# A fixed order for every engine up to the first feed-forward step of an attention and mixture kernel

## The chip, the cores and the metric

The kernel runs on one core of one Trainium2 chip. The metric is device time in microseconds of one execution. A core has a matrix engine (TensorE, PE in the profile; PEld is its weight load), VectorE (DVE), ScalarE (ACT), GpSimd (POOL) and SyncE (SP), which here only issues DMAs. Each engine works through its own list of instructions in order; semaphores hold an instruction back until what it needs is done.

## The reference, cut to what matters

```python
def _attn_ref(q, k, v, mem_k, mem_v):            # (4, 8, 768, 64), 8 memory rows
    for c in range(24):                          # chunks of 32 queries
        k_full = concat(mem_k, k[c_start - 16:c_end + 8])     # cut at both ends
        scores = scale * q_c @ k_full.T
        a = exp(scores - max(scores)); a = a / (sum(a) + 1e-09)
        out[:, :, c_start:c_end] = a @ v_full

def _moe_ref(x, w_in, w_out, s, b):              # x (3072, 512), d_ff 2048
    r = maximum(x @ w_in, 0.0)
    return (s * (r * r) + b) @ w_out

def _moe2_ref(x, phi, w1, w2):                   # 8 experts of 4 slots
    logits = x @ phi
    slot_input = softmax(logits, axis=0).T @ x
    slot_out[e] = maximum(slot_input[e] @ w1[e], 0.0) @ w2[e]
    return softmax(logits, axis=1) @ slot_out
```

The weights w_in and w_out arrive in 64-bit floats and are turned into 32-bit ones on the chip.

## The kernel before

The 3072 tokens are worked in six blocks j of 512 tokens. The attention of a block is four units, one for each pair of heads, so unit u is pair u % 4 of block u // 4. A unit is a chain over all engines: `spread_q` (S, first block only: the two heads of q are copied to where their zeros have been cleared, one half of the partitions by ScalarE, one by VectorE), `att_qk` (A: 32 matmul records into one bank, then VectorE clears masked columns of that bank), `att_soft` (F: row maximum and subtraction on VectorE, exponential on ScalarE, row sum, epsilon and reciprocal on VectorE, the normalising multiply on Pool in the start and on VectorE later), `att_tr` (T or t: four transposes on PE, two copies into `pb`), `att_pv` (P: matmuls with v, then x's high part on ScalarE and its low part on VectorE).

The feed-forward part takes 96 steps n, 16 a block; step n works on slice f = n % 16 of d_ff. `mm_h` multiplies x with wi, `make_g` makes s r^2 + b, `mm_y` multiplies it with wo. Each fp32 operand is split into a high and a low part (`split_wi`, `split_wo`: ScalarE rounds, VectorE subtracts in the first 16 steps, Pool later), and a product is three passes: high x high, high x low, low x high. In the first block each half of a weight slice is also decoded from 64 bits: `w_load` brings a half (512 KB) into a staging tile; `w_decode` clamps it on VectorE, makes two pieces on ScalarE and joins them on VectorE. The halves come in the order (0, 0), (0, 1), (1, 0), ..., where (f, 0) is wi and (f, 1) is wo of slice f. `START` decodes some halves, and steps 0 to 13 two each. mm_h(n) needs half (n, 0), mm_y(n) needs (n, 1).

`START` is a string of tokens: q, k, v, c and w load; z issues warm-up products for PE that nothing reads; I is `split_wi`; H is one quarter of step 0's `mm_h`; D decodes one half; y hands four spent tiles to the staging list, and w9 loads halves into all that is free. Everything stands in `tc.manual_schedule` for PE and SP: these two keep the order in which the code issues. The order on ScalarE, VectorE and Pool is made by a planner at build time, which takes the code's order as priority and a model of durations for when things are ready; on the chip that order is fixed. After `START` come steps 0, 1, ...: splits for the next step, `mm_h`, `make_g`, two decodes, the attention of the next block (`bg`, from step 1 on) and `mm_y` of the step before. So the quarter H3, in step 0, and `mm_h(1)` follow the start on PE, then A4, the scores of unit 4, the first of the next block.

## Time and profile before

| | us |
|---|---|
| median of three runs | 697.64 (697.57 to 698.52) |
| profiled execution | 697.7 |
| its span on the core | 695.9 |
| PE busy | 675.7 |
| DVE busy | 357.7 |
| ACT busy | 353.6 |
| POOL busy | 216.7 |

The profile's times are counted from the start of the span; 1.8 us of the execution lie around it. PE's first instruction starts at 1.31 us. Busy time of PE is that of pipelined matmuls, whose ends are modelled. The granted clock of PE is a share of 2.4 GHz and stands at 0.5 or 1.0 at any moment; a stretch shows the mean. Engines other than PE have idle time that costs nothing as long as PE doesn't wait for them.

### The profile page before, as it was taken

To read this page: it belongs to the slowest core of one execution; us is meant where nothing else is said; L and a number is where in the kernel's file an instruction comes from. 1 tells how busy PE (TensorE), PEld (TensorE's weight loads), DVE (VectorE), ACT (ScalarE), POOL (GpSimd) and SP (SyncE) were. 2 spreads that over 40 slices of the span, in tenths; PEclk is the share of its full clock that TensorE was granted. 3 is DMA by queue.
4 is the path that set the end of the run, shared out by engine and by line. 5 is a ranking of instruction groups with operands and counts; after the bars stand their busy time and mean duration, and the time that the engine had idled before them with its cause. 6 is when DMAs were issued, how large, how long until landed. Compare 5 with 4: busy or idle time off the path is not lost.

```text
span 695.9 us, 12228 instructions
## 1 busy us (share of the span) xinstructions
PE 675.7 (97%) x4953; PEld 533.3 (77%) x4953; DVE 357.7 (51%) x644; ACT 353.6 (51%) x628; POOL 216.7 (31%) x178
## 2 busy tenths in 40 slices
PE   7599999999999999999999999999999999999995
PEld 4488888888788888788888788888788888787353
DVE  5689997446534456544445444554553332223233
ACT  4779894544444445444445444545444544444332
POOL 4100000343344334334434334434334444441000
PEclk9799999999999999999999999999999999999998
DMA  9998802702201211211120221120123523628998
GB/s 348 389 336 328 270 40 91 284 32 80 91 16 77 91 42 50 91 52 64 68 75 18 91 67 56 61 91 1 62 84 129 211 92 91 211 92 272 237 294 348
DMA packets 47032, 94.38 MB, mean 136 GB/s; under 512 B 2944, under 2 KB 27520, under 8 KB 46976
## 3 DMA queue, kind: packets, MB, share of 16 engines
q1 hardware_dynamic: 46976, 93.60, 39.3%
q8 instruction: 39, 0.64, 0.4%
q14 instruction: 17, 0.14, 0.1%
HBM read 87.30 MB, written 6.29 MB: 134 GB/s over the span
## 4 chain that ended last, share of the span: by engine, by line
PE 95%; DVE 2%; ACT 1%; POOL 1%; issue 0%; POOLq 0%; DVEq 0%; ACTq 0%
PE bank L292 39%; PE bank L272 38%; PE bank L221 4%; PE bank L181 3%; PE bank L686 2%; PE bank L643 2%; PE bank L207 2%; PE bank L336 1%; PE bank L712 1%; PE bank L314 1%; PE bank L352 1%; PE bank L504 1%; PE bank L390 0%; POOL rt L201 0%; PE bank L662 0%
## 5 line engine op out<-in xcount | busy, mean ns | idle before, releaser
L292 PE MATMUL bank<-g,wo 128*128 128x512 f32 x1152 | 285.2, 396 | 0.0
L272 PE MATMUL bank<-x,wi 128*128 128x512 f32 x1152 | 278.6, 391 | 0.0
L272 PEld LDWEIGHTS bank<-x,wi 128*128 128x128 f32 x1152 | 217.1, 189 | 45.2
L292 PEld LDWEIGHTS bank<-g,wo 128*128 128x128 f32 x1152 | 211.1, 188 | 48.9 <-ACT wi L259 4.2
L279 DVE SCALAR_TENSOR_TENSOR rt<-bank,cons,rt 128x512 f32<-128x512 f32 x96 | 72.0, 750 | 228.3 <-ACT rt L278 228.1
L265 POOL TENSOR_TENSOR wo<-w,wo 128x512 fp32r<-128x512 f32 x80 | 103.2, 1290 | 204.9 <-ACT wo L264 200.9
L260 POOL TENSOR_TENSOR wi<-w,wi 128x512 fp32r<-128x512 f32 x80 | 103.4, 1293 | 188.8 <-ACT wi L259 188.8
L259 ACT ACTIVATE wi<-w 128x512 fp32r<-128x512 f32 x96 | 60.5, 630 | 148.3 <-PE bank L272 144.8
L280 ACT ACTIVATE g<-rt,cons 128x512 fp32r<-128x512 f32 x96 | 69.4, 723 | 42.6 <-DVE rt L279 41.3
L264 ACT ACTIVATE wo<-w 128x512 fp32r<-128x512 f32 x96 | 60.3, 628 | 55.2 <-PE bank L292 53.5
L281 DVE SCALAR_TENSOR_TENSOR g<-rt,cons,g 128x512 fp32r<-128x512 f32 x96 | 72.0, 750 | 27.3 <-ACT g L280 24.5
L278 ACT ACTIVATE rt<-bank 128x512 f32<-128x512 f32 x96 | 55.8, 581 | 5.4 <-PE bank L272 5.2
L197 ACT ACTIVATE ep<-ep 128x512 f32<-128x512 f32 x22 | 13.8, 627 | 30.1 <-DVE ep L196 30.1
L221 PEld LDWEIGHTS bank<-pb,v 128*64 128x64 f32 x704 | 22.3, 138 | 7.1 <-issue 6.7
L181 PEld LDWEIGHTS bank<-k,q 128*64 128x64 f32 x704 | 22.4, 138 | 5.6 <-issue 4.5
L181 PE MATMUL bank<-k,q 128*64 128x64 f32 x704 | 24.7, 223 | 1.7 <-ACT ep L197 1.7
L221 PE MATMUL bank<-pb,v 128*64 128x64 f32 x704 | 25.3, 225 | 0.0
L198 DVE TENSOR_REDUCE ast<-ep 128x8 f32<-128x512 f32 x22 | 15.1, 685 | 9.8 <-ACT ep L197 9.7
L225 DVE TENSOR_TENSOR x<-bank,x 128x512 fp32r<-128x512 f32 x24 | 16.5, 688 | 0.6 <-ACT x L224 0.5
L224 ACT ACTIVATE x<-bank 128x512 fp32r<-128x512 f32 x24 | 14.3, 596 | 4.9 <-PE bank L221 2.5
L195 DVE TENSOR_REDUCE ast<-bank 128x8 f32<-128x512 f32 x24 | 16.4, 683 | 0.4
L199 DVE TENSOR_SCALAR ast<-ast 128x8 f32<-128x8 f32 x24 | 15.9, 664 | 0.7
(237 smaller groups left out, 522.6 us busy)
## 6 DMA issues: line engine op xcount, KB each, us to landing
k<-kd SPq DMA_DIRECT2D x22, 512.0 KB, 6.1
sp<-wd SPq DMA_DIRECT2D x22, 512.0 KB, 8.8
v<-vd SPq DMA_DIRECT2D x22, 512.0 KB, 3.9
q<-qd SPq DMA_DIRECT2D x20, 512.0 KB, 5.3
w<-e1d SPq DMA_DIRECT2D x10, 512.0 KB, 3.4
out<-w SPq DMA_DIRECT2D x9, 512.0 KB, 6.2
sp<-e1d SPq DMA_DIRECT2D x7, 512.0 KB, 7.9
sp<-e2d SPq DMA_DIRECT2D x7, 512.0 KB, 7.2
```

Of the source, the lines that this page charges most:

```text
L181: pe.matmul(S[64 * par:64 * par + 64, 2 * i + z, :], lhsT=qt[:, c].rearrange("p h n -> p (h n)"), rhs=kt[:, c, :], start=True, stop=True)
L221: pe.matmul(b[64 * h:64 * h + 64, 64 * m:64 * m + 64], lhsT=vt[:, m, h, :], rhs=pb[:, m // 2, m % 2, h].rearrange("p z n -> p (z n)"), sta ...
L259: act.activation(out=r32(t[:, 0]), in_=raw, func=AF.Copy)
L260: (dve if n < NF else pool).tensor_tensor(out=r32(t[:, 1]), in0=raw, in1=t[:, 0], op=ALU.subtract)
L264: act.activation(out=r32(t[:, 0]), in_=raw, func=AF.Copy)
L265: (dve if n < NF else pool).tensor_tensor(out=r32(t[:, 1]), in0=raw, in1=t[:, 0], op=ALU.subtract)
L272: pe.matmul(HB[n % 2], lhsT=r32(w[:, a, kt, :]), rhs=r32(x[:, b]), start=(kt == 0 and i == 0), stop=(kt == 3 and i == 2))
L278: act.activation(out=r, in_=HB[n % 2], func=AF.Relu, scale=1.0 / WSCALE ** 2)
L279: dve.scalar_tensor_tensor(out=t, in0=HB[n % 2], scalar=s_col, in1=r, op0=ALU.mult, op1=ALU.mult)
L280: act.activation(out=r32(g[:, 0]), in_=t, func=AF.Identity, bias=b_col)
L281: dve.scalar_tensor_tensor(out=r32(g[:, 1]), in0=t, scalar=b_col, in1=g[:, 0], op0=ALU.add, op1=ALU.subtract)
L292: pe.matmul(YB[dt], lhsT=r32(w[:, a, dt * 128:dt * 128 + 128]), rhs=r32(g[:, b]), start=(f == 0 and i == 0), stop=(f == NF - 1 and i == 2))
```

## The change

The start's order is now fixed on ScalarE, VectorE and Pool too: the loop over the tokens stands in a second `manual_schedule` for these three, inside the one for PE and SP. Where instructions from outside the region (steps 0, 1, ...) fall among those of the region is still the planner's. To make the order finer, several functions are cut in two: `att_soft` into `att_exp` (m: clears, maximum, subtraction, exponential) and `att_norm` (n: sums and multiply), with the clears moved out of `att_qk` into m; x's low part out of `att_pv` into `att_low` (x); `w_decode` into `w_begin` (D: clamp and ScalarE's pieces) and `w_end` (E: the join); `split_wi` into `wi_high` (I) and `wi_low` (i). The VectorE half of S1, S2 and S3 moves to Pool. T0 now copies with ScalarE alone, T3 with ScalarE and VectorE. One warm-up product of the three at the start goes, and the others stand elsewhere. Halves of weights are loaded and decoded in the order (0, 0), (1, 0), (0, 1), (2, 0), (1, 1), (3, 0), .... The start decodes four halves, as before; w9 now comes after the last of them.

```diff
--- before.py
+++ after.py
@@ -22,9 +22,9 @@
 NEG = -3.0e38
 EPS = 1e-9
 START = (
-    "q0 k0 w1 c0 q1 k1 q2 k2 v0 w1 q3 k3 v1 w1 v2 v3 w1 "
-    "z3 S0 A0 F0 z1 S1 D0 A1 z1 S2 t0 z1 A2 P0 F1 S3 T1 F2 "
-    "I0 A3 k4 w1 q4 w1 k5 P1 v4 w1 T2 q5 H0 P2 F3 T3 P3 y0 H1 w9 H2 D0 v5 D0 D0"
+    "q0 k0 q1 k1 w1 c0 q2 k2 v0 q3 k3 v1 w1 v2 w1 v3 w1 "
+    "z2 S0 A0 z1 S1 A1 m0 n0 D0 S2 m1 A2 E0 T0 I0 n1 S3 m2 z1 P0 T1 A3 i0 n2 x0 m3 P1 T2 D1 n3 x1 E1 H0 P2 "
+    "k4 w1 q4 w1 k5 v4 w1 q5 T3 H1 P3 x2 D2 H2 x3 E2 D3 E3 y0 w9 v5"
 )
 WSCALE = 256.0
 PARTS = ((0, 256), (256, 128), (384, 128))
@@ -164,14 +164,13 @@
     def spread_q(u):
         t, src = qv(u), qsv(u)
         act.activation(out=t[0:64, :, 0, :], in_=src[0:64], func=AF.Copy)
-        dve.tensor_copy(t[64:128, :, 1, :], src[64:128])
+        (pool if u else dve).tensor_copy(t[64:128, :, 1, :], src[64:128])
 
...
     def att_qk(u, b):
-        j = u // NHP
         S = b.rearrange("p (t n) -> p t n", t=8)
         qt, kt = qv(u), kv(u)
         for i in range(4):
@@ -180,6 +179,11 @@
                     c = 4 * i + 2 * par + z
                     pe.matmul(S[64 * par:64 * par + 64, 2 * i + z, :], lhsT=qt[:, c].rearrange("p h n -> p (h n)"), rhs=kt[:, c, :],
                               start=True, stop=True)
+
+    def att_exp(u, b):
+        S = b.rearrange("p (t n) -> p t n", t=8)
+        E, mx = epv(u), ast[u % 2][:, 0, :]
+        j = u // NHP
         for c in range(CB):
             gc = j * CB + c
             par, t = (c % 4) // 2, 2 * (c // 4) + c % 2
@@ -187,14 +191,12 @@
                 dve.memset(S[64 * par:64 * par + 64, t, 8:24], NEG)
             if gc % 24 == 23:
                 dve.memset(S[64 * par:64 * par + 64, t, 56:64], NEG)
-
-    def att_soft(u, b, last=None):
-        S = b.rearrange("p (t n) -> p t n", t=8)
-        E = epv(u)
-        mx, sm = ast[u % 2][:, 0, :], ast[u % 2][:, 1, :]
         dve.tensor_reduce(out=mx, in_=S, axis=AX.X, op=ALU.max)
         dve.tensor_tensor(out=E, in0=S, in1=mx.unsqueeze(2).to_broadcast([P, 8, 64]), op=ALU.subtract)
         act.activation(out=E, in_=E, func=AF.Exp, scale=0.125)
+
+    def att_norm(u, last=None):
+        E, sm = epv(u), ast[u % 2][:, 1, :]
         dve.tensor_reduce(out=sm, in_=E, axis=AX.X, op=ALU.add)
         dve.tensor_scalar(out=sm, in0=sm, scalar1=EPS, scalar2=None, op0=ALU.add)
         dve.reciprocal(out=sm, in_=sm)
@@ -222,10 +224,14 @@
                           rhs=pb[:, m // 2, m % 2, h].rearrange("p z n -> p (z n)"), start=True, stop=True)
         xt = hl(X[j % 2][hp])
         act.activation(out=r32(xt[:, 0]), in_=b, func=AF.Copy)
+
+    def att_low(u, b):
+        j, hp = divmod(u, NHP)
+        xt = hl(X[j % 2][hp])
         dve.tensor_tensor(out=r32(xt[:, 1]), in0=b, in1=xt[:, 0], op=ALU.subtract)
 
 
-    halves = [(f, h) for f in range(NF) for h in range(2)]
+    halves = [(0, 0)] + [x for f in range(NF - 1) for x in ((f + 1, 0), (f, 1))] + [(NF - 1, 1)]
     stage_free = list(SPARE)
     stage_full = []
     hnext = [0]
@@ -239,25 +245,47 @@
             sp.dma_start(out=t.bitcast(U32), in_=wd[f][:, 512 * h:512 * h + 512].bitcast(U32))
             stage_full.append((f, h, t))
 
-    def w_decode():
-        f, h, t = stage_full.pop(0)
...
+    half_done = []
+
+    def w_begin():
+        f, h, t = stage_full.pop(0)
+        low, high, hv, top, dst = w_views(f, h, t)
         dve.tensor_scalar(out=hv, in0=hv, scalar1=-EXP_TOP, scalar2=EXP_TOP, op0=ALU.max, op1=ALU.min)
         act.activation(out=hv, in_=hv, func=AF.Prelu, scale=EXP_SHIFT, alpha=SIGN_SHIFT)
         act.activation(out=low, in_=top, func=AF.Copy, scale=1.0 / 32.0, bias=-31.0 / 64.0)
+        half_done.append((f, h, t))
+
+    def w_end():
+        f, h, t = half_done.pop(0)
+        low, high, hv, top, dst = w_views(f, h, t)
         dve.scalar_tensor_tensor(out=dst, in0=high, scalar=3, in1=low, op0=ALU.logical_shift_left,
                                  op1=ALU.bitwise_or)
         stage_free.append(t)
 
-
-    def split_wi(n):
+    def w_decode():
+        w_begin()
+        w_end()
+
+
+    def wi_high(n):
         t, raw = hl(WI[n % 2]), W[n % NF][:, 0:512]
         act.activation(out=r32(t[:, 0]), in_=raw, func=AF.Copy)
+
+    def wi_low(n):
+        t, raw = hl(WI[n % 2]), W[n % NF][:, 0:512]
         (dve if n < NF else pool).tensor_tensor(out=r32(t[:, 1]), in0=raw, in1=t[:, 0], op=ALU.subtract)
+
+    def split_wi(n):
+        wi_high(n)
+        wi_low(n)
 
     def split_wo(n):
         t, raw = hl(WO[n % 2]), W[n % NF][:, 512:1024]
...
@@ -518,6 +549,10 @@
             sbk[u] = sbank()
             att_qk(u, sbk[u])
 
+        def s_pv(u):
+            sbk[u] = sbank()
+            att_pv(u, sbk[u])
+
 
         steps = {
             "c": lambda _: sp.dma_start(out=cons, in_=cd),
@@ -527,19 +562,22 @@
             "S": spread_q,
             "w": w_load,
             "z": keep_warm,
-            "t": lambda u: att_tr(u, sbank()),
             "A": s_qk,
-            "F": lambda u: att_soft(u, sbk[u], pool),
-            "T": lambda u: att_tr(u, sbank(), True),
-            "P": lambda u: att_pv(u, sbank()),
-            "D": lambda _: w_decode(),
-            "I": split_wi,
-            "O": split_wo,
+            "m": lambda u: att_exp(u, sbk[u]),
+            "n": lambda u: att_norm(u, pool),
+            "T": lambda u: att_tr(u, sbank(), u < 3),
+            "P": s_pv,
+            "x": lambda u: att_low(u, sbk[u]),
+            "D": lambda _: w_begin(),
+            "E": lambda _: w_end(),
+            "I": wi_high,
+            "i": wi_low,
             "H": lambda kt: mm_h(0, (kt,)),
             "y": lambda _: stage_free.extend(YT + Y),
         }
-        for token in START.split():
-            steps[token[0]](int(token[1:]))
+        with tc.manual_schedule(engines={mybir.EngineType.Activation, mybir.EngineType.DVE, mybir.EngineType.Pool}):
+            for token in START.split():
+                steps[token[0]](int(token[1:]))
 
 
         for n in range(NSTEP):
```

## Rows read from the trace of the kernel before

**Rows 1.** The page's first part: busy us, share of the span, instructions.

```profile
PE 675.7 (97%) x4953; PEld 533.3 (77%) x4953; DVE 357.7 (51%) x644; ACT 353.6 (51%) x628; POOL 216.7 (31%) x178
```

**Rows 2.** Stretches of 10 us: each engine's busy us, TensorE clock, DMA share, GB/s.

```profile
30.00:40.00 10.00, 8.32 (x56) 6.82 (x56) 4.85 (x9) 5.91 (x12) 0.27 (x1) 0.67 0.81 288
...
40.00:50.00 10.00, 10.00 (x72) 8.14 (x71) 9.68 (x21) 7.93 (x14) 0.00 (x0) 1.00 1.02 387
...
100.00:110.00 10.00, 10.00 (x100) 8.30 (x99) 9.77 (x20) 6.28 (x11) 0.00 (x0) 1.00 0.43 148
```

**Rows 3.** The chain of waits to 50 us: start us, us, piece, instructions.

```profile
1.31 5.08 PE bank L504 x6
...
34.77 5.84 PE bank L272 x21
...
40.61 1.08 PE bank L181 x32
...
44.64 2.72 PE bank L272 x12
```

**Rows 4.** Waits to 40.6 us: who waited for whom, us, times, longest.

```profile
PE bank L207 <- POOL rt L201: 5.8, 2, 3.4
```

**Rows 5.** Groups to 40.6 us: line, engine, form, count, busy us, mean ns, idle.

```profile
L197 ACT ACTIVATE ep<-ep 128x512 f32<-128x512 f32 x2 | 1.3, 630 | 2.8 <-DVE ep L196 2.8
...
L198 DVE TENSOR_REDUCE ast<-ep 128x8 f32<-128x512 f32 x2 | 1.4, 682 | 0.7 <-ACT ep L197 0.7
...
L199 DVE TENSOR_SCALAR ast<-ast 128x8 f32<-128x8 f32 x4 | 0.7, 170 | 0.1
...
L200 DVE RECIPROCAL ast<-ast 128x8 f32<-128x8 f32 x4 | 0.8, 199 | 0.0
...
L201 POOL TENSOR_TENSOR ep<-ep,ast 128x512 f32<-128x512 f32 x2 | 2.1, 1042 | 9.3 <-DVE ast L200 9.3
...
L212 ACT ACTIVATE pb<-bank 64x512 f32<-64x512 f32 x3 | 1.8, 592 | 0.1
...
L225 DVE TENSOR_TENSOR x<-bank,x 128x512 fp32r<-128x512 f32 x4 | 2.7, 686 | 0.5 <-ACT x L224 0.5
...
L249 DVE TENSOR_SCALAR sp<-sp 128x512 f32<-128x512 f32 x6 | 2.7, 449 | 2.0 <-DMA sp<-wd 2.0
...
L251 ACT ACTIVATE sp<-sp 128x512 uint32<-128x512 uint8 x6 | 4.0, 670 | 2.2 <-DMA sp<-wd 2.2
...
L252 DVE SCALAR_TENSOR_TENSOR w<-sp 128x512 uint32<-128x512 uint32 x6 | 4.1, 690 | 1.4 <-ACT sp L250 1.2 <-ACT sp L251 0.2
...
L512 POOL MEMSET pb<- 64x512 f32 x2 | 1.0, 517 | 0.1
```

**Rows 6.** Transfers issued at 1.18 (k0), 11.1 (v3), 22.17 (seventh half): us to landing.

```profile
k<-kd SPq DMA_DIRECT2D x1, 512.0 KB, 3.8
...
yt<-vd SPq DMA_DIRECT2D x1, 512.0 KB, 11.0
...
sp<-wd SPq DMA_DIRECT2D x1, 512.0 KB, 10.6
```

**Rows 7.** PE's instructions in order: start us, us, line; T0, P1, T2, P3.

```profile
13.49 0.66 PE L207 MATMUL bank<-cons,ep 128*128 128x128 f32 x4 [1.02 <-POOL ep L201]
...
19.33 1.15 PE L221 MATMUL bank<-pb,v 128*64 128x64 f32 x32
...
22.88 1.11 PE L207 MATMUL bank<-cons,rt 128*128 128x128 f32 x4 [2.40 <-POOL rt L201]
...
32.80 1.97 PE L221 MATMUL bank<-pb,yt 128*64 128x64 f32 x32 [1.36 <-ACT pb L212]
```

**Rows 8.** Instructions in order, 28 to 39 us: wi's low parts, Pool's multiply.

```profile
28.28 0.69 DVE L260 TENSOR_TENSOR wi<-w,wi 128x512 fp32r<-128x512 f32 x1
...
29.22 1.05 POOL L201 TENSOR_TENSOR rt<-rt,ast 128x512 f32<-128x512 f32 x1 [6.40 <-DVE ast L200]
...
38.37 0.69 DVE L260 TENSOR_TENSOR wi<-w,wi 128x512 fp32r<-128x512 f32 x1 [1.89 <-ACT wi L259]
```

More of the change, by code (lines that the diff above doesn't have):

```diff
@@ L240, in w_load, with w_views @@
             stage_full.append((f, h, t))
-    def w_decode():
-        f, h, t = stage_full.pop(0)
+    def w_views(f, h, t):
         u = t.bitcast(U32).rearrange("p (n w) -> p n w", w=2)
@@ L248, in w_decode @@
         dst = W[f][:, 512 * h:512 * h + 512].bitcast(U32)
+        return low, high, hv, top, dst
+    half_done = []
+    def w_begin():
+        f, h, t = stage_full.pop(0)
+        low, high, hv, top, dst = w_views(f, h, t)
         dve.tensor_scalar(out=hv, in0=hv, scalar1=-EXP_TOP, scalar2=EXP_TOP, op0=ALU.max, op1=ALU.min)
@@ L468, in run_bg @@
                 load_k(a + 2)
-            att_soft(a, b)
+            att_exp(a, b)
+            att_norm(a)
         elif k == "tr":
@@ L472, in run_bg @@
         elif k == "pv":
-            att_pv(a, mbank())
+            b = mbank()
+            att_pv(a, b)
+            att_low(a, b)
             if a + 2 < NB * NHP:
```

## The prediction, made before the change was run

> **What bounds the kernel now.** I read the engine table first: TensorE is busy for 97% of the span [rows 1]. An average hides where the rest is, so the next view is the stretches of 10 us: the reader is to see that PE is busy for 10.00 of 10 us from 40 us on, but for 8.32 in the stretch before, where its granted clock is 0.67 [rows 2]. The chain of waits says the same in one line: after P3 (the fourth unit's attention output) the first-step products H1 to H3 and all of step 1's mm_h run as one block of 21 from 34.77, and the next piece, the fifth unit's scores A4, begins at 40.61; from there the chain is PE to the end [rows 3]. So PE's work after A4 is fixed, and an edit of the start is worth what it moves A4's begin, less what PE has to wait later because the other engines are not yet as far.
>
> What held the start is in the waits: PE's transposes (L207) waited 5.8 us in two pieces for Pool's normalising multiply, which came late because VectorE had other work ahead of what the multiply needs [rows 4]: wi(1)'s low part starts at 28.28, unit 3's multiply only at 29.22 [rows 8]. VectorE is only 4.85 us busy between 30 and 40 us [rows 2]: it was not short of time there, its order was wrong for the times at which things really arrived.
>
> **The change, part by part.** The new order is fixed on all five engines, so its chain can be added up. Durations are those of [rows 5] unless another group is named; ScalarE's 128x512 pieces with no row there, and S2 and S3, are put at the exponential's 0.63, VectorE's maximum and subtraction at the sum's 0.68. A hand-over from engine to engine is put at about 0.05 us, from VectorE to Pool at 0.15. Times are from the span's start.
>
> Warm-up. One of three opening products goes. The six instructions of z3 took 5.08 us, 0.85 each [rows 3]; four end at 1.31 + 3.4 = 4.7. k0 lands 3.8 us after its issue at 1.18 [rows 6], 4.98. A0 starts at 5.0 instead of 6.39; it runs at the slower pace of these instructions, I put 1.4, between 1.15 and 1.97, the ends that P1 and P3, of as many products, show [rows 7], and ends at 6.4.
>
> Unit 0 and the first decode: clear (put at 0.07), maximum and subtraction: 7.9; exponential 0.63: 8.55; sum, epsilon, reciprocal 0.68 + 0.17 + 0.20: 9.7. Now the clamp, 0.45, stands on VectorE ahead of unit 1's maximum: 10.15; ScalarE's two decode pieces, 0.67 each: 11.5; and only behind them S2, 0.63: 12.2. A2 stands ahead of T0 on PE, so T0, whose input Pool has ready at 10.9, waits: A2 (1.15, as P1 [rows 7]) 12.2 to 13.35, T0 (0.66) to 14.0. This part is no gain: T0 began at 13.49 before [rows 7].
>
> The middle. ScalarE is the chain: two copies of T0 (0.59 each) 15.25, the high part of wi(0) 15.9, S3 16.55, exponential of unit 2 17.2. VectorE: sum, epsilon, reciprocal 18.3, x0's low part (0.69) 19.0, clear, maximum and subtraction of unit 3 20.5. ScalarE: exponential 21.15, x1's high part 21.75, two copies of T2 22.95. PE: P2 (1.15) 24.15, T3 24.8. Pool's multiply for unit 3 is ready at 21.15 + 1.05 + 0.15 + 1.04 = 23.4, hidden behind P2; without that cover it would cost 1.04.
>
> The tail. Decode D1 on ScalarE 24.3, x2's high part 24.9, its copy of T3 25.5; on VectorE E1 25.05, its copy of T3 25.75. P3 25.8 to 26.95. v3 lands at 11.1 + 11.0 = 22.1 [rows 6]; the loads ahead of the last v and the fourth w hold the same bytes in both orders, so it hides behind the chain with 3.7 us to spare. x3's high part 27.6, low part 28.3. H3 is three products of 0.227 (2.72 for twelve [rows 3]): 29.0. Step 1's mm_h: 31.7. So A4 would begin at 31.7 instead of 40.61: 8.9 us.
>
> From this I take off two things. First, D2 and D3 (ScalarE 2.7, VectorE 2.3) and whatever the planner slips in between the fixed instructions lie around P3 and x3. The region fixes the order inside it, not where instructions of step 0 and 1 fall among it. wi(1) is decoded by 25.05; if its two halves go into the idle time beside P3 they cost 0 to 0.6; if they come behind D3 and E3, the line is D2's pieces 28.95, E2 29.65, D3's clamp 30.1 and pieces 31.5, the high part 32.15, E3 32.2, the low part 32.9; mm_h(1) wants that from its third product on, so A4 starts at 32.9 - 0.45 + 2.72 = 35.2, 3.5 later. I take 0.6, since in the trace of before the planner did put wi(1)'s low part (28.28) ahead of unit 3's multiply (29.22) [rows 8]. Second, PE is idle from A1's end (8.4) to A2 (12.2), the longest pause in the new order. Before, the pause between 20.5 and 22.9 was followed by the lower clock: T2 took 1.11 there against 0.66 for T0, and P3 1.97 against 1.15 for P1 [rows 7]. I charge 0.7 between 0 (clock stays) and 1.2 (A2, T0 and the warm-up product at the lower level). A4 at 33.0: 7.6 us earlier.
>
> The Trainium skill, "TensorE: Matmul & The Clock Gate", "Why this matters for your kernels", has a rule against this order: a long pause between bursts of matmuls sends the array back to half clock. By that rule the full 1.2 would be charged, and the sum is 0.5 less. T2's 1.11 agrees with it; how long a pause it takes here, these rows don't show.
>
> Pool's copies. One half each of S1 to S3 moves from VectorE to Pool, whose rows hold no copy. The nearest are its memset of a 64x512 tile, 0.52, and its multiply of 128x512, 1.04; I take 0.6, near the memset, which handles as many elements. Below zero is excluded: it's an added Pool instruction. S2's runs from 10.9, S3's from 15.2, and ScalarE's halves end at 12.2 and 16.55, so up to 1.3 each is hidden; above that it would cost one for one.
>
> What is given back. At A4 before, VectorE had finished six decoded halves [rows 5] and the low part of wi(2) (38.37) [rows 8]; in the new order it has four, and no wi(2): 2 x (0.45 + 0.69) + 0.69 = 2.97 us behind. VectorE is 9.68 of 10 us busy from 40 us and still 9.77 at 100 to 110 [rows 2], so it works with nothing to spare, though ahead of need, as PE never waits. The need order of halves gives back 1.14, since mm_h(3) needs six halves in it and seven before. Of the remaining 1.8 I charge PE with 1.0, between 0 and 2.9.
>
> The queues. SP, which has kept to a fixed order before too, stands still at w9 until E2 and E3 free two staging tiles (about 32 us), with v5 behind it, which unit 5 needs much later. The other moved loads wait for things long done. Seven w halves are in by 22.17 + 10.6 = 32.8 [rows 6], as before. Nothing is charged. The splitting of functions (maximum from sums, high from low) adds no instruction.
>
> **Sum.** 7.6 - 1.0 = 6.6 us. The profiled execution took 697.7, a span of 695.9 with 1.8 around it; it stands 0.06 above the median of 697.64. Forecast: 697.7 - 6.6 = 691.1, or 691.0 against the median. With the bounds named: best 8.9 - 0 = 688.7, and with all the small charges 8.9 - 0.6 - 1.2 - 2.9 = 4.2, 693.4.
>
> **Rivals.**
> Late split: wi(1) stands behind D3 and E3. A4 at 35.2 and 0.7 for the clock: 4.7 us, less 1.0: 694.0. For it: both are earlier in program order. Against: the planner's order before.
>
> Slow clock: PE stays at the lower level in most of the start. Then P0, P2, P3 and T0, T2, T3, H3 and half of mm_h(1) run at the lower level, of which T0 0.45, P2 and P3 0.8 each, T3 0.45, H3 0.7 and 0.9 of mm_h(1) lie on the chain: 4.1 in place of the 0.7 that I charge, so 3.2 us are left: 694.4. For it: 0.67 at 30 to 40 us [rows 2]; against: PE's pauses after 12.2 are at most 1.6 us by the chain above.
>
> Given back: VectorE becomes the bound in steps 1 to 9 and PE ends where it did, 697.5. Against: VectorE begins its steady stretch 8 us earlier and has 3 us more to do.
>
> Slower: an instruction of steps 0 to 2 that the planner slips in among the fixed ones waits for a transfer that on the chip lands later than planned; on an engine in order everything fixed queues behind it. If the clamp of the seventh half (lands 32.8) stands ahead of unit 3's maximum (19.0), the remaining 12.7 us to A4 start at 32.8: A4 at 45.5, 4.9 later than before: 702.5. It decides from a hold to 27.9 on. Against: before, of the six decodes up to A4 one waited for its transfer, 2.2 us [rows 5], and that was the first.
>
> The order does nothing: were the region not to hold the engines, the old interleaving stays, 697 to 698; I count it with "given back".
>
> More gain: VectorE has time in hand and the clock never falls, 688.
>
> **Chances.** Forecast 0.56 (own range 688.7 to 693.4), late split 0.14, slow clock 0.09, given back 0.08, slower 0.10, more gain 0.03. A measurement here tells about 0.2% (1.4 us) from no change. Faster 0.82, same 0.08, slower 0.10. The range for 8 in 10 leaves out slower, given back and some of the best: 688.0 to 695.5.
>
> **What would show it.** PE's block with H3 begins near 29 us and A4 near 33; T0 not earlier than 13.5 to 15; granted clock under 1.00 for a stretch after 12 us; ScalarE without idle time of over 1.7 us between 14 and 28 us; PE waits of 0 to 2 us in sum between 33 and 90 us, ended by VectorE's wo or wi; Pool's copies under 1.2 us. I am wrong if A4 begins after 36, if a fixed instruction waits for a w transfer, or if PE's waits after A4 exceed 3 us.

## The result, and the profile after

The changed kernel takes 691.88 us (median of four runs, 691.29 to 692.85) beside 697.98 us for the kernel before on the same chip (697.57 to 698.52): a ratio of 0.9913, 95% interval 0.9900 to 0.9925. That is 6.1 us, or 0.9%, more than the 0.2% that a measurement tells from no change. The forecast was 691.0, range 688.0 to 695.5. The profiled execution, the shortest of the four, took 691.29, a span of 689.3, 6.6 us under the span before.

The page's first part: busy us, share of the span, instructions. PE is busy for 3.9 us less than in [rows 1], with four instructions fewer: these are two warm-up products of six, where the text above has one. The rest I put down to the clock, which the stretches show.

```profile
PE 671.8 (97%) x4949; PEld 530.8 (77%) x4949; DVE 355.4 (52%) x641; ACT 352.8 (51%) x628; POOL 218.6 (32%) x181
```

Stretches of 10 us of the kernel after (busy us of PE, PEld, VectorE, ScalarE, Pool, each with its instructions; PE's granted clock; DMA share; GB/s).

```profile
0.00:10.00 10.00, 7.05 (x70) 3.53 (x70) 3.80 (x11) 3.27 (x5) 5.85 (x15) 1.00 0.80 290
10.00:20.00 10.00, 7.36 (x120) 5.95 (x122) 7.18 (x16) 6.67 (x12) 3.85 (x5) 0.83 1.02 408
20.00:30.00 10.00, 7.44 (x111) 5.61 (x106) 7.29 (x15) 8.01 (x14) 1.28 (x2) 1.00 1.03 412
30.00:40.00 10.00, 10.00 (x72) 8.11 (x71) 9.85 (x20) 9.47 (x18) 0.00 (x0) 1.00 1.02 405
40.00:50.00 10.00, 8.92 (x69) 7.11 (x68) 9.94 (x21) 10.00 (x20) 0.00 (x0) 1.00 1.01 396
```

Against [rows 2]: in 30 to 40 us PE was 8.32 us busy at a clock of 0.67, now it is 10.00 at 1.00. VectorE is up from 4.85 to 9.85 there, since its steady stretch now begins at 30. In 40 to 50 us the sign turns: PE had no idle time there before and has 1.08 us now, with VectorE at 9.94 and ScalarE at 10.00 of 10.

PE's instructions in order (start us, us, line, [idle before <- what ended it]). In turn: A0, A1, A2, T0, P3, H3 with mm_h(1), A4, T4.

```profile
5.00 1.15 PE L180 MATMUL bank<-k,q 128*64 128x64 f32 x32
...
7.92 1.15 PE L180 MATMUL bank<-k,q 128*64 128x64 f32 x32 [0.72 <-DMA k<-kd]
11.83 1.98 PE L180 MATMUL bank<-y,q 128*64 128x64 f32 x32 [2.75 <-DMA y<-kd]
13.74 1.12 PE L209 MATMUL bank<-cons,ep 128*128 128x128 f32 x4
...
26.74 1.15 PE L223 MATMUL bank<-pb,yt 128*64 128x64 f32 x32 [0.77 <-DVE pb L216]
...
29.34 3.48 PE L300 MATMUL bank<-x,wi 128*128 128x512 f32 x14 [0.23 <-DVE x L231]
32.75 1.15 PE L180 MATMUL bank<-k,q 128*64 128x64 f32 x32
...
46.09 0.66 PE L209 MATMUL bank<-cons,ep 128*128 128x128 f32 x4 [1.08 <-DVE ep L203]
```

A4 begins at 32.75 where it began at 40.61 [rows 3]: 7.86 us earlier. The one wait that PE has between A4 and the last part of the kernel is the 1.08 us ahead of T4. 7.86 - 1.08 is 6.78; the span is 6.6 shorter. The two waits of 5.8 us for Pool's multiply [rows 4] are gone. The waits of PE from 30 us to the end (who for whom, us, times, longest):

```profile
PE bank L209 <- DVE ep L203: 1.1, 1, 1.1
...
```

Those left out, 0.9 us and less, lie in the last layer, which neither the change nor the experiments touch.

### The profile page after: what moved, and what is told of

It reads as the page before. It is cut to its first block, busy times and chain, and to the rows that moved or that the text cites. A ratio compares the mean times of both kernels' runs of the same rounds, so it can differ in the third digit from the quotient of the medians.

```text
span 689.3 us, 12225 instructions
## 1 busy us (share of the span) xinstructions
PE 671.8 (97%) x4949; PEld 530.8 (77%) x4949; DVE 355.4 (52%) x641; ACT 352.8 (51%) x628; POOL 218.6 (32%) x181
## 4 chain that ended last, share of the span: by engine, by line
PE 92%; ACT 2%; DVE 2%; DMA 1%; issue 1%; SPq 0%; DVEq 0%; ACTq 0%
PE bank L320 38%; PE bank L300 36%; PE bank L223 3%; PE bank L180 3%; PE bank L724 2%; PE bank L681 2%; PE bank L209 1%; PE bank L364 1%; DMA y<-kd 1%; PE bank L750 1%; PE bank L342 1%; PE bank L380 1%; PE bank L418 0%; DVE w L269 0%; ACT sp L262 0%
## 5 line engine op out<-in xcount | busy, mean ns | idle before, releaser
L307 DVE SCALAR_TENSOR_TENSOR rt<-bank,cons,rt 128x512 f32<-128x512 f32 x96 | 72.0, 750 | 228.2 <-ACT rt L306 228.1
L262 ACT ACTIVATE sp<-sp 128x512 f32<-128x512 f32 x24 | 15.9, 677 | 3.0 <-DVE sp L261 3.0
L269 DVE SCALAR_TENSOR_TENSOR w<-sp 128x512 uint32<-128x512 uint32 x24 | 16.2, 684 | 1.8 <-ACT sp L263 1.6
```

The lines of the kernel that those rows point to most:

```text
L307: dve.scalar_tensor_tensor(out=t, in0=HB[n % 2], scalar=s_col, in1=r, op0=ALU.mult, op1=ALU.mult)
```

## The experiments

My theory: the fixed region moves A4 by some 8 us, all of it by order alone, and part comes back as waits of PE behind VectorE, which has no time to spare while halves are decoded. The rivals: the planner would do the same with the finer tokens, or the need order of halves brings the gain (tested in e1, e2, e3, e8); Pool's spreading carries weight (e4); the clock in the start, not the order, sets what is left (e5); what is given back is VectorE's load and could be moved to Pool, or is only T4's place (e6, e7, e9, e10, e11).

Each run stands beside the kernel before on its own chip; ratios are to that, with a 95% interval. "A4" is where PE's 32 scores of unit 4 begin.

**after_again.** The changed kernel once more.

> The changed kernel once more, beside the others of this call. Expected as measured: 691.3 to 692.5, A4 at 32.7 to 33.4, T0 at 1.12 us at the lower clock, one PE wait of about 1.1 us ahead of T4.

Measured: 691.82 us (691.39 to 693.08) beside 698.19, 0.9913 (0.9899 to 0.9926). The profiled execution, at 693.08, was the longest of them and shows what spreads: the stretch of 10 to 20 us, then A1 and A2.

```profile
10.00:20.00 10.00, 6.91 (x81) 4.95 (x78) 6.89 (x13) 5.63 (x10) 3.30 (x4) 0.66 1.03 409
```

```profile
8.97 1.15 PE L180 MATMUL bank<-k,q 128*64 128x64 f32 x32 [1.74 <-DMA k<-kd]
13.22 1.97 PE L180 MATMUL bank<-y,q 128*64 128x64 f32 x32 [3.09 <-ACT q L166]
```

k1 landed a microsecond later than in the first profile (A1 at 8.97, not 7.92), PE's pause ahead of A2 grew to 3.09, and the clock in that stretch was 0.66, not 0.83. A4 came at 34.30, 1.55 later; the execution took 1.8 us more. So nearly all of the difference between these two executions arises in the first 20 us.

A2's row names ScalarE's half of S2 here, where the first profile names k2. VectorE's clamp of the first half of the weights and ScalarE's S2, both of this execution:

```profile
10.42 0.95 DVE L261 TENSOR_SCALAR sp<-sp 128x512 f32<-128x512 f32 x1 [0.55 <-DMA sp<-wd]
```

```profile
12.51 0.61 ACT L166 ACTIVATE q<-w 64x512 f32<-64x512 f32 x1
```

In the first profile the clamp began at 9.49 without a wait and S2 ended at 11.64. Here the half, issued at 2.59, landed 7.81 us later, at 10.4. The clamp, fixed at that place by the region, waited 0.55 us for it and then took 0.95 instead of 0.38, beside Pool's multiply of unit 0 (10.05 to 11.09). The decode pieces and S2 stand behind it, and S2 ended at 13.12. k2 had landed only at about 13.0 (issued at 4.01, 9.0 us to landing), so A2 had two late lines, and both come from the transfers.

**e1_no_region.** The changed kernel without its region, so that its tokens are fixed on PE and SP alone.

```diff
-        with tc.manual_schedule(engines={mybir.EngineType.Activation, mybir.EngineType.DVE, mybir.EngineType.Pool}):
-            for token in START.split():
-                steps[token[0]](int(token[1:]))
+        for token in START.split():
+            steps[token[0]](int(token[1:]))
```

> The changed kernel without the inner region, so that the planner orders ScalarE, VectorE and Pool again; tokens, cut functions, load order and need order stay. Theory (the fixed order of the three engines brings most of the gain): in the list that the planner makes, VectorE has the clamps of the third to sixth half ahead of x2's or x3's low part, and the sixth half lands at about 29 us, so x3's low part comes no earlier than 30; A4 begins at 35 to 37 against 32.8, part of which VectorE gives back later since more halves are then decoded: 693 to 695.5. Rival (the new token order alone, as priority, does it): A4 within 1 us of 32.8, 691 to 692.5. Rival (only the order matters and the planner undoes it): A4 at 40, 697 to 698.

Measured: 697.50 us beside 698.77, 0.998 (0.9968 to 0.9993); A4 at 41.11. The gain all but goes, more than my theory gave and as the last rival has it: the planner makes of the new tokens an order about as slow as the old one. ScalarE's, VectorE's and PE's instructions in order show how it begins:

```profile
19.33 0.68 ACT L263 ACTIVATE sp<-sp 128x512 uint32<-128x512 uint8 x1 [2.44 <-DMA sp<-wd]
19.91 0.57 ACT L212 ACTIVATE pb<-bank 64x512 f32<-64x512 f32 x1
```

```profile
19.33 0.43 DVE L261 TENSOR_SCALAR sp<-sp 128x512 f32<-128x512 f32 x1 [1.44 <-DMA sp<-wd]
19.67 0.19 DVE L202 RECIPROCAL ast<-ast 128x8 f32<-128x8 f32 x1
```

```profile
21.15 1.98 PE L223 MATMUL bank<-pb,v 128*64 128x64 f32 x32 [4.37 <-ACT pb L214]
```

The second half's decode was placed ahead of T0's copies on ScalarE and ahead of unit 2's reciprocal on VectorE. Its transfer landed at 19.3; both engines stood until then with ready work behind, PE waited 4.37 us for the copies, and P0 began at 21.15 instead of 16.15. This is the mechanism of my rival "slower", here in the planner's order. These 5.0 us are the larger part of the 8.4 by which A4 comes later; the rest comes behind P0 (P3 at 34.05 instead of 26.74), and I haven't taken it apart.

**e2_old_tokens_fixed.** The kernel before with nothing but the region around its old tokens.

```diff
-        for token in START.split():
-            steps[token[0]](int(token[1:]))
+        with tc.manual_schedule(engines={mybir.EngineType.Activation, mybir.EngineType.DVE, mybir.EngineType.Pool}):
+            for token in START.split():
+                steps[token[0]](int(token[1:]))
```

> The kernel before with the inner region alone: the old tokens and whole functions, issued in the code's order on all engines. Theory (the gain is the cut of the functions and their new places; fixing as such gives nothing): sums wait for exponentials with the next unit's maximum behind them, and the clamp, splits and normalising stand in line; unit after unit is serial, A4 begins at 45 to 51 against 40.6: 702 to 708. Rival (the planner is what cost the time, any fixed order mends it): A4 before 36, under 694.

Measured: 714.19 us beside 698.77, 1.0216 (1.0189 to 1.0243); A4 at 56.02. The direction was expected, the size not: 15 us. Pieces of the chain of waits (start us, us, piece):

```profile
18.65 0.69 DVE x L225
19.34 0.61 DVE ast L195
...
33.49 0.69 DVE x L225
34.19 0.60 DVE ast L195
```

Unit 1's maximum (L195) stands behind x0's low part (L225) on VectorE, because the old token P0 holds that low part and comes ahead of F1. So unit 1's softmax begins when unit 0 has been through P0, and unit 3's maximum stands in the same way behind unit 2's low part: the units run nearly one after another. In the changed kernel the cut of `att_pv` into P and x, and of `att_soft` into m and n, lets a maximum go ahead. e2 keeps the old order of the tokens as well; whether the uncut functions in another fixed order, F1 ahead of P0 for one, would gain was not run.

**e8_old_need_order.** The kernel before with nothing but the need order of halves.

```diff
-    halves = [(f, h) for f in range(NF) for h in range(2)]
+    halves = [(0, 0)] + [x for f in range(NF - 1) for x in ((f + 1, 0), (f, 1))] + [(NF - 1, 1)]
```

> The kernel before with the need order of halves alone. Theory (before, the start hangs on the planner's order of VectorE and Pool, not on when a half is decoded): P3 and the block behind it within 1 us of 34.8, A4 within 1 us of 40.6, 697 to 698.5. Rival (need order by itself brings part of the gain, as its removal from the changed kernel cost 2 us): A4 1.5 to 2.5 earlier, 695.3 to 696.3.

Measured: 698.39 us beside 698.19, 1.0005 (0.999 to 1.002); A4 at 40.88. Alone it brings nothing that can be measured: PE still waits 5.8 us in two pieces for Pool's multiply, as in [rows 4].

**e3_halves_in_turn.** The changed kernel with the old order of halves.

```diff
-    halves = [(0, 0)] + [x for f in range(NF - 1) for x in ((f + 1, 0), (f, 1))] + [(NF - 1, 1)]
+    halves = [(f, h) for f in range(NF) for h in range(2)]
```

> The changed kernel with the halves of the weights loaded and decoded in the old order (0, 0), (0, 1), (1, 0), (1, 1): the need order alone is undone. Theory (need order matters for mm_h(1), whose half (1, 0) would now be the third decode, joined only behind x3's low part, at about 29.7): wi(1)'s low part ends at about 31.5, mm_h(1) ends near 33.8, A4 begins at 33.8 to 34.5 against 32.8, PE's waits after it as long as now or 0.5 more: 692.8 to 694.2. Rival (need order is worth nothing in the start, halves are decoded ahead of need anyway): A4 within 0.3 of 32.8, 691.6 to 692.2.

Measured: 693.46 us beside 698.16, 0.9932 (0.9915 to 0.9948); A4 at 36.36, later than I expected, while the time is in what I gave. PE, mm_h(1):

```profile
31.22 0.73 PE L300 MATMUL bank<-x,wi 128*128 128x512 f32 x2 [1.26 <-ACT wi L280]
32.52 3.91 PE L300 MATMUL bank<-x,wi 128*128 128x512 f32 x10 [0.57 <-DVE wi L284]
```

(1, 0) is now the third half to be decoded, so mm_h(1) waits 1.83 us for wi(1), and the ten products after that take 3.91 us, at a granted clock of 0.83 between 30 and 40 us. The wait ahead of T4 is gone in exchange. The difference to the changed kernel's medians is 1.6 us; the two intervals overlap a little, so that the need order is worth something beside the region is likely, and its size is not settled.

**e4_spread_on_dve.** The changed kernel with S1 to S3 back on VectorE.

```diff
-        (pool if u else dve).tensor_copy(t[64:128, :, 1, :], src[64:128])
+        dve.tensor_copy(t[64:128, :, 1, :], src[64:128])
```

> The changed kernel with the lower halves of S1 to S3 back on VectorE: Pool's part of the change alone is undone. Theory (Pool's 0.61 us copies lie beside ScalarE's halves, and VectorE has 0.4 us to spare at each of the three places): T0 and P0 within 0.4 of now, A4 within 0.3 of 32.8, 691.6 to 692.3. Rival (VectorE is tight there, the copy of 0.43 delays unit 1's and 2's maximum and all behind it): A4 0.5 to 1.3 later, 692.4 to 693.2.

Measured: 690.96 us beside 698.16, 0.9906 (0.9885 to 0.9926), below both ranges that I gave; A4 at 32.79, a wait of 1.0 ahead of T4. Pool's spreading is worth nothing that can be measured; VectorE hides these copies too.

**e5_warm_gap.** Three warm-up products fill PE's pause between A1 and A2.

```diff
-    "z2 S0 A0 z1 S1 A1 m0 n0 D0 ...
+    "z2 S0 A0 z1 S1 A1 z3 m0 n0 D0 ...
```

> The changed kernel with three more warm-up products (0.86 us each) in PE's pause between A1 and A2. Theory (the pause lowers the clock, and A2 and T0 at the lower level are on the chain): granted clock stays 1.00 from 10 to 20 us, A2 takes 1.15 instead of 1.98, T0 0.66 instead of 1.12, T0 ends 1.2 earlier, A4 begins 0.6 to 1.2 earlier than 32.8, and 690.7 to 691.4 against 691.9. Rival (ScalarE's line, not T0, is the chain there): A2 and T0 shorten, A4 moves by under 0.2, 691.8 to 692.0. Rival (the products run into A2): A2 begins later than 11.9 and nothing is gained.

Measured: 691.16 us (691.02 to 691.87) beside 698.77, 0.9892 (0.9867 to 0.9916). The stretch of 10 to 20 us, PE's A2, and PE's waits between 30 and 110 us:

```profile
10.00:20.00 10.00, 8.58 (x143) 5.77 (x141) 8.11 (x19) 6.78 (x12) 4.38 (x5) 1.00 1.03 414
```

```profile
12.50 1.15 PE L180 MATMUL bank<-y,q 128*64 128x64 f32 x32 [0.40 <-ACT ep L196]
13.58 0.66 PE L209 MATMUL bank<-cons,ep 128*128 128x128 f32 x4
```

```profile
PE bank L320 <- ACT g L308: 0.8, 1, 0.8
PE bank L209 <- DVE ep L203: 0.7, 1, 0.7
```

With the pause filled the clock stays at 1.00, and A2 and T0 take 1.15 and 0.66 us. A2 itself began later than in the first profile of the changed kernel, at 12.50: k2, issued at 4.01, took 8.3 us to land. So the distance from A2 to A4 tells more than A4's date. It is 19.62 us here, and 19.61 and 19.68 in e7 and e11, which fill the pause in the same way, against 20.92 in the first profile and 21.08 in after_again: the 1.3 us of the clock reach A4. A4 came at 32.12, 0.63 earlier than in the first profile. PE's waits afterwards are 1.5 us instead of 1.1, and the span is 689.2 against 689.3. The clock term of the sum is real; most of what came earlier is given back behind ScalarE's make_g and VectorE.

**e6_lows_on_pool.** The low parts of wi and wo on Pool from step 2 on, to take load off VectorE.

```diff
-        (dve if n < NF else pool).tensor_tensor(out=r32(t[:, 1]), in0=raw, in1=t[:, 0], op=ALU.subtract)
+        (dve if n < 2 else pool).tensor_tensor(out=r32(t[:, 1]), in0=raw, in1=t[:, 0], op=ALU.subtract)
```

(in `wi_low` and in `split_wo`).

> The changed kernel with the low parts of wi and wo on Pool from step 2 on instead of step 16 (Pool is idle from 30 to 110 us). Theory (PE's wait of 1.1 us for unit 4's multiply is VectorE's backlog, the price of starting early): VectorE loses 1.38 us a step, the wait ahead of T4 falls to 0 to 0.3, A4 stays near 32.8, 690.7 to 691.2. Rival (the wait comes from the planner's order, not from VectorE's load): the wait stays or turns up at another place, 691.6 to 692.2. Rival (Pool and VectorE disturb each other): VectorE's subtractions beside Pool's take over 0.9 us, and PE waits as long or longer, 692 to 694.

Measured: 698.70 us beside 698.77, 0.9994 (0.9978 to 1.0011): the whole gain lost, beyond every range that I gave, with A4 at 33.28. PE's waits between 30 and 110 us add up to 6.4 us instead of 1.1, and its clock was 0.83 from 90 to 100 us. Groups by form of VectorE, 38 to 100 us (count, busy us, mean ns of one, idle), first of e6, then of the changed kernel:

```profile
L269 DVE SCALAR_TENSOR_TENSOR w<-sp 128x512 uint32<-128x512 uint32 x17 | 13.8, 818 | 1.6 <-ACT sp L263 1.2 <-ACT sp L262 0.4
L309 DVE SCALAR_TENSOR_TENSOR g<-rt,cons,g 128x512 fp32r<-128x512 f32 x9 | 9.2, 1022 | 0.1
L261 DVE TENSOR_SCALAR sp<-sp 128x512 f32<-128x512 f32 x17 | 9.1, 555 | 0.0
L307 DVE SCALAR_TENSOR_TENSOR rt<-bank,cons,rt 128x512 f32<-128x512 f32 x8 | 5.9, 744 | 1.0 <-ACT rt L306 0.8
```

```profile
L269 DVE SCALAR_TENSOR_TENSOR w<-sp 128x512 uint32<-128x512 uint32 x16 | 10.7, 682 | 0.1
L309 DVE SCALAR_TENSOR_TENSOR g<-rt,cons,g 128x512 fp32r<-128x512 f32 x11 | 8.2, 748 | 0.1
L307 DVE SCALAR_TENSOR_TENSOR rt<-bank,cons,rt 128x512 f32<-128x512 f32 x10 | 7.5, 748 | 0.1
...
L261 DVE TENSOR_SCALAR sp<-sp 128x512 f32<-128x512 f32 x17 | 6.5, 419 | 0.0
```

And Pool's, of e6:

```profile
L284 POOL TENSOR_TENSOR wi<-w,wi 128x512 fp32r<-128x512 f32 x10 | 14.0, 1402 | 21.6 <-ACT wi L280 18.2 <-DVE rt L307 3.4
```

Beside Pool's subtractions VectorE's join of two SBUF operands goes from 682 to 818 ns, make_g's last step from 748 to 1022, the clamp in place from 419 to 555. L307, which reads one of its operands from a PSUM bank, stays at 744 to 748. On top of that, a low part takes 1402 ns on Pool and 687 on VectorE, so that wi and wo come later. The Trainium skill, "SBUF — State Buffer", "Who interferes with whom", says that a VectorE instruction with two SBUF inputs contends with a Pool instruction that reads SBUF, and one with at most one SBUF input, outside certain modes, doesn't. The join, make_g's last step and L307 agree with it; the clamp, with one SBUF input, agrees only if it ran in one of those modes, which no row shows.

**e7_warm_pool_clamp.** e5, and the clamps of the decodes of steps 0 to 13 on Pool.

```diff
-    def w_begin():
+    def w_begin(eng=dve):
...
-        dve.tensor_scalar(out=hv, in0=hv, scalar1=-EXP_TOP, scalar2=EXP_TOP, op0=ALU.max, op1=ALU.min)
+        eng.tensor_scalar(out=hv, in0=hv, scalar1=-EXP_TOP, scalar2=EXP_TOP, op0=ALU.max, op1=ALU.min)
...
-        w_begin()
+        w_begin(pool)
```

> The kernel with the filled pause (three products between A1 and A2) and the clamps of the decodes in steps 0 to 13 on Pool. The subtractions on Pool took 1.3 to 1.7 us, and VectorE's instructions with two SBUF operands beside them up to 1.77 instead of 0.75. Theory (Pool and VectorE take turns at operands in SBUF also for one-operand work): clamps take 0.6 to 1.2 on Pool, some VectorE instructions beside them are lengthened by as much, PE's waits after A4 are 1 to 4 us: 691 to 694. Rival (only two-operand work on Pool disturbs): VectorE's pieces stay at 0.69 and 0.75, the waits of 1.55 us of the filled pause go to 0 to 0.5, 689.6 to 690.4.

Measured: 692.51 us beside 698.19, 0.9923 (0.9909 to 0.9936); A4 at 32.21, then 1.9 us of wait ahead of T4. Pool's groups by form, 30 to 110 us:

```profile
L261 POOL TENSOR_SCALAR sp<-sp 128x512 f32<-128x512 f32 x19 | 40.4, 2162 | 2.6 <-DMA sp<-wd 2.6
```

A clamp that takes VectorE 0.42 us takes Pool 2.16, where I expected 1.2 at most. VectorE is rid of it, but its joins went from 0.68 to between 0.77 and 1.02 us in the groups of that stretch. No gain.

**e9_no_clamp.** The changed kernel without the clamps of those 28 decodes (part of the computation is left out).

```diff
-    def w_begin():
+    def w_begin(clamp=True):
...
+        if clamp:
...
-        w_begin()
+        w_begin(False)
```

> The changed kernel in which the decodes of steps 0 to 13 leave out the clamp on VectorE (28 of 32 halves; values outside the clamp's range would come out wrong). Theory (PE's wait of 1.1 us ahead of T4 is VectorE's load in the first steps): VectorE has 0.84 us less a step, the wait falls to 0 to 0.3, A4 stays within 0.5 of 32.8: 690.3 to 691.0. Rival (the planner's order makes the wait, load doesn't matter): a wait of 0.8 to 1.5 stays there or elsewhere in steps 0 to 6, 691.6 to 692.3.

Measured: 691.48 us beside 698.16, 0.9912 (0.9894 to 0.9931); A4 at 33.46. The wait ahead of T4 no longer shows. The chain of waits to T4:

```profile
45.68 0.70 DVE ep L203
46.42 0.66 PE bank L209 x4
```

Unit 4's multiply (L203) ends at 46.4, where it ended at 46.0 in the changed kernel: with the clamps gone VectorE delivers it no earlier. T4 doesn't wait because PE comes 1.4 us later, at 46.42; in the changed kernel it was free for T4 at 45.01 and then waited 1.08. Of the 1.4 us, 0.71 is the later A4, in part since the planner now put a join (28.72) ahead of x3's low part (29.32 instead of 28.60) and H3 waits 0.5 us for it. The first mm_y waits another 0.5 for make_g. So the run neither shows that less load on VectorE takes the wait away nor measures what the load costs, since the planner's order around it changed too. The time lies between the two ranges that I gave.

**e10_t4_later.** T4 and P4 one step later.

```diff
-            bg[n0 + 2].append(("tr", u))
-            bg[n0 + (4 if hp in (1, 2) else 3)].append(("pv", u))
+            late = 1 if u == 4 else 0
+            bg[n0 + 2 + late].append(("tr", u))
+            bg[n0 + late + (4 if hp in (1, 2) else 3)].append(("pv", u))
```

> The changed kernel with T4 and P4 (the transposes and output of the next block's first unit) one step later. Theory (VectorE as a whole is behind, so a wait taken away at one place comes back at another): PE's waits from 33 to 100 us stay 0.5 to 1.1 in sum, 691.2 to 692.0. Rival (VectorE is late for this one date only): no wait of PE between 33 and 100 us, A4 unchanged, 690.6 to 691.0.

Measured: 690.82 us (690.24 to 691.94) beside 698.16, 0.9897 (0.9882 to 0.9912). PE's waits between 30 and 110 us:

```profile
PE bank L223 <- ACT y L262: 0.5, 1, 0.5
...
PE bank L209 <- DVE ep L203: 0.2, 1, 0.2
```

T4 waits 0.2 us at its new place, and a wait of 0.5 turns up ahead of an attention output, for ScalarE's decode piece (the line left out is H3's 0.2, ahead of A4). The wait moved and shrank. The two waits, 0.7 us in sum, are what the theory gave, while the time lies in the rival's range, so that the run doesn't decide between them.

**e11_warm_t4_later.** e5 and e10 together.

```diff
-    "z2 S0 A0 z1 S1 A1 m0 n0 D0 ...
+    "z2 S0 A0 z1 S1 A1 z3 m0 n0 D0 ...
...
-            bg[n0 + 2].append(("tr", u))
+            bg[n0 + 2 + late].append(("tr", u))
```

> Both of the edits that gained: the filled pause and T4, P4 one step later. Theory (an earlier A4 is given back by VectorE in the first steps): A4 at about 32.1, PE's waits from 32 to 65 us 0.7 to 1.6 in sum, 690.3 to 691.3, little or nothing below either edit alone. Rival (the two are independent): A4 at 32.1 and waits of 0.7 at most, 690.0 to 690.3.

Measured: 691.17 us (690.98 to 691.25) beside 698.19, 0.99 (0.9886 to 0.9913); A4 at 32.09, PE's waits 0.8 and 0.8. The two edits don't add. e4, e5, e10 and e11 lie between 690.8 and 691.2 us, and none is told apart from the changed kernel by its interval. The spread is 0.9 us in e5 and 0.3 in e11, over four runs each, against 1.6 and 1.7 in the two sets of the changed kernel; but e7, where the pause is filled too, spreads over 1.5, so that a steadier time is not shown.

## Why the prediction was right, step by step

**The bound.** A4's begin set the time, as forecast: 7.86 us earlier, less 1.08 us of new wait, is the span's 6.6 within 0.2. The sum had 7.6 and 1.0.

**Warm-up and unit 0.** A0 started at 5.00, as worked out. It ran at full pace, 1.15 instead of the 1.4 that I took. In other executions with the same opening it took up to 1.98 (e7), so that 1.4 was a fair middle and the gain of 0.25 luck. The reciprocal of unit 0 ended at 9.58 (forecast 9.7).

**A2.** Here the sum had one line of two. I had A2 at 12.2 behind S2, which ScalarE does after the first decode. S2 was done by 11.64; A2 began at 11.83, and its row names the landing of k2. The chain of waits says the same:

```profile
4.13 7.57 DMA y<-kd
```

k2 is issued at 4.13 and lands 7.57 us later, at 11.70, as the eighth transfer of its queue; A1 waited for k1 in the same way, to 7.92, where the sum has about 7.2. I had priced the landing of k0, v3 and the seventh half, not of the loads between. An estimate from the bytes gives the size. Up to and with k2 the queue holds 3074 KB (three q of 256, three k of 512, a half of 512, the constants of 258), 3.15 MB; by the stretches of after, 2.90 MB are moved in the first 10 us and 408 GB/s from there, so k2 would be in at 10.6 if the queue's loads moved strictly one after another, and with the next loads on their way beside it it landed at 11.7. The two lines end within 0.1 us of each other. Over the profiled executions with this start, A2's row names k2 in five (after, e4, e6, e9, e10), S2 in four (after_again, e3, e7, e11), and neither in e5.

The S2 line hangs on a transfer too, for which I charged nothing. The change moved the first half of the weights behind q1 and k1 in the queue. In the kernel before it landed 4.6 us after its issue at 1.65, at about 6.2. Now it landed 6.5 us after 2.58, at 9.1, only 0.4 ahead of the fixed clamp at 9.49, and in after_again 0.55 after VectorE was ready for it.

**The clock.** I charged 0.7 of at most 1.2 us. A2 took 1.98 and T0 1.12 instead of 1.15 and 0.66, which is 1.29: the whole bound. This is the term of the sum that was too small. T0 ended at 14.86, against 14.0 without any charge, since A2 came 0.4 before the forecast. e5, which keeps the clock at 1.00, went from A2 to A4 in 1.3 us less. So the rule of the Trainium skill that I weighed ("TensorE: Matmul & The Clock Gate", "Why this matters for your kernels") was the better guide on this term: the trace agrees that after PE's pause of 2.75 us the array was at the lower level, and after 3.09 us in after_again too.

**The middle and the tail.** T0's end lay 0.86 behind the sum without charges, and A4 at 32.75 1.05 behind its 31.7, so that the distance between them came out nearly as forecast. Within it two differences cancel. Down to ScalarE's copy of T3, which ended at 25.96 instead of 25.5, the chain caught up 0.4 us. Then VectorE's copy of T3, which the sum has beside ScalarE's, came only after it:

```profile
25.37 0.59 ACT L212 ACTIVATE pb<-bank 64x512 f32<-64x512 f32 x1
...
26.00 0.69 DVE L216 COPY pb<-bank 64x512 f32<-64x512 f32 x1 [0.50 <-ACT pb L212]
```

That step was wrong and cost 0.5: P3 at 26.74 lay 0.94 behind, and H3's block, which began at 29.34, 1.04. ScalarE had an idle time of 2.73 us up to 14.89, waiting for T0, of which 0.89 lie in the stretch of 14 to 28 us that I named; behind it the longest was 1.63, ahead of unit 3's exponential (forecast under 1.7). The rival "slow clock" didn't come about: 1.00 from 20 us on.

**The late split.** I charged 0.6 for wi(1) beside P3; it cost nothing. ScalarE's and VectorE's rows, wi(1)'s high part with the decode piece behind it, then its low part with x3's:

```profile
25.87 0.62 ACT L280 ACTIVATE wi<-w 128x512 fp32r<-128x512 f32 x1
26.65 0.71 ACT L263 ACTIVATE sp<-sp 128x512 uint32<-128x512 uint8 x1 [0.17 <-DMA sp<-wd]
```

```profile
27.66 0.69 DVE L284 TENSOR_TENSOR wi<-w,wi 128x512 fp32r<-128x512 f32 x1
...
28.60 0.68 DVE L231 TENSOR_TENSOR x<-bank,x 128x512 fp32r<-128x512 f32 x1
```

The planner put both ahead of x3, into the idle time beside P3, as in the trace of before [rows 8]. So 0.6 too much here and about 0.6 too little on the clock cancel, which is luck; the 33.0 for A4 is right with these two terms off.

**Slower.** One of my signs of being wrong came up: a fixed instruction did wait for a w transfer. The third decode's piece waited for 0.17 us, with x3's high part behind it and 0.59 us of idle time before that: no cost. In after_again the first clamp waited 0.55 us, on the line to A2. e1 shows the same mechanism with 2.44 us on ScalarE and 4.37 on PE. So the rival's mechanism is at work in the fixed order too, at 0.2 to 0.6 us and not at the 4.9 that I gave it.

**Pool's copies.** Forecast 0.6; measured, by form, up to 30 us:

```profile
L167 POOL COPY q<-w 64x512 f32<-64x512 f32 x2 | 1.2, 607 | 0.1
```

They are hidden, and e4 shows that VectorE would have hidden them as well.

**Given back.** 1.1 us at one place, ended by VectorE's multiply of unit 4 (L203), against 1.0 charged. The size is right; the place wasn't the one that I named (wo or wi), and that VectorE alone lacks the time, as my sum has it, isn't shown. VectorE is 9.85 and 9.94 of 10 us busy, but ScalarE is as full in 40 to 50 us (10.00). The chain of waits to T4 runs over ScalarE from 39.1 to 43.6 us, and only its end is VectorE's:

```profile
42.95 0.62 ACT g L308
...
45.43 0.61 DVE ep L203
```

In e9, with VectorE's clamps gone, the multiply came no earlier; in e5, e10 and e11 ScalarE ends part of the waits. How much belongs to each engine and how much to the planner's order stays open.

**The need order.** I reckoned its 1.14 us from VectorE's work. e3 lost 1.6 us in the medians, but by another route: mm_h(1) waits 1.83 us for wi(1) in the start. The need order keeps the region's own line short. Whether it also relieves the stretch after it e3 can't tell: it had no wait ahead of T4, but its A4 came 3.6 us later, which gave VectorE that much more time.

**What of the change brings it.** Not the finer tokens in their new order alone (e1: 0.2%), not the region alone (e2: 2.2% slower), not the need order alone (e8: nothing), and not Pool's copies (e4). The gain takes both, tokens cut finely and their order fixed; the need order adds perhaps 0.2%. That it lies in not putting work behind a transfer that lands later is read from e1's rows; the fixed order isn't free of such places either. What the cut and what the new order of tokens is worth by itself was not separated.

## What to carry to other kernels

Where an engine's instructions stand in a planned order, read each engine's rows for one that waits for a transfer with ready work behind it; fixing the order there paid, in this kernel, only with functions cut so that every piece can stand where it is needed. When the start gets shorter, add up the bytes ahead of every load that the new line passes, above all of loads that the change moves back in their queue, since transfers can become the next bound. And look at how full the other engines are right after it: in e5 and e11 most of what an A4 earlier by 0.6 us won came back as waits. Two terms that are off can leave a sum right, so compare the steps, not only the total.

## What the runs showed of the hardware that I had not expected

A clamp with two constants in place, 128x512, takes Pool 2.16 us (e7) and VectorE 0.42, a factor of 5, while Pool copies 64x512 in 0.607, so that one Pool instruction's time says little of another's. Beside Pool's subtractions (e6) VectorE's join, make_g's last step and clamp, all on SBUF operands, took 0.14 to 0.27 us longer on the mean, the one-input clamp among them (419 to 555 ns). And the same start shows a granted clock of 0.83 in one execution and 0.66 in another for the same 10 us, where PE's pause ahead of A2 was 2.75 us and ended at 11.83 in the one, and was 3.09 and ended at 13.22 in the other.
